# Layer 2's token rows in slot order: 16 direct stores in place of 16 scatters, no rows of zeros

## The chip, the core and the metric

One of the eight cores of a Trainium2 chip runs the kernel. The metric is the time of one execution on the device in microseconds (us), input in HBM to output in HBM. A core has five engines with a program each: PE (TensorE, matrix products; PEld is its load of weights), DVE (VectorE), ACT (ScalarE), POOL (GpSimd) and SP (SyncE, which here only issues transfers). Transfers run on 16 DMA engines; SP, ACT and POOL issue them. SBUF is the core's memory of 128 partitions, PSUM the one that PE writes.

## What is computed

Tokens pass through a retention (a linear attention with a decay for each head), a mixture of 8 experts without a limit, and a second mixture whose experts hold at most 384 tokens each, first come first served:

```python
for t in range(S):                                    # B=2, H=8, S=768, 64 wide
    state = gamma * state + einsum('bhd,bhe->bhde', k[:, :, t], v[:, :, t])
    y[:, :, t] = scale * einsum('bhd,bhde->bhe', q[:, :, t], state)
# _moe_ref: N=1536 tokens, D=512, E=8, F=1024
expert_idx = argmax(x @ w_gate);  gate_w = softmax(x @ w_gate)[expert_idx]
out[mask_e] = gate_w * (maximum(x[mask_e] @ w1[e], 0) @ w2[e])
# _moe2_ref: the same, but token i is kept only if its expert has had fewer than `capacity` tokens; else out[i] = 0
```

## The kernel before

**Three stages.** From 0 to about 66 us the retention runs over 12 tiles of 128 tokens (`for n in range(NT)`). PE, DVE and POOL work on tile n while SP loads the q, k and v of tile n+3 (`a_load`). Each tile ends as rows of 520 f32, 512 values of the token and its 8 logits for layer 1, which ACT stores to the DRAM array `x1d` (line 564). From 66 to about 250 us comes the first mixture (`li == 0`), from there to the end the second (`li == 1`). The two are called layer 1 and layer 2 here.

**One expert.** A layer takes its experts in an order found at run time and gives each a fixed number of slots (`CAPS`: 240, 220, 208, 200, 192, 188, 184, 176 in layer 1). So that PE works on full rows, an expert's tokens are gathered from DRAM by an indirect DMA on POOL (`take`, line 347): 128 rows and a rest of 48 to 112, called the halves r0 and r1. Weights and tokens are split into a high and a low part: SP loads f32 weights `st`, ACT makes `whi` (line 159), DVE makes `wlo = st - whi` (line 170). The hidden layer runs in four groups: PE makes `h` (800, 801), ACT copies `hb` (785), DVE adds into `hs` (786), ACT makes the high part of relu (811), DVE the low part (812), both into tile `h`. Then PE makes `y` from them (844, 845) in two passes, ACT copies `yb`, DVE adds `yt` (785, 786).

**Rows of layer 2.** `comb` brings `yt` of an expert back to rows: four matmuls into `cb` (1334), on DVE the logits (1340) times the gate (1342), on ACT the 512 values times the gate (1347) into `row`, one of four buffers. Then `scatter(x2d, ...)` (line 321, POOL) sends each row to `x2d` at its token's number; slots that hold no token have an index out of range and are left out. All this is in a list `pend`, of which `between` runs pieces inside the next expert: r0 of expert j in the first hidden group of expert j+1, r1 in the second. Only expert 7's two halves come after its own products. `rou` then ranks the rows for layer 2 (`route_tile`, lines 204 to 234) on DVE and PE.

**What else touches `x2d`.** Twelve stores of a tile of zeros clear it first (`clear`, line 661): seven in the retention behind a tile's loads, five inside layer 1's expert 0, all on SP. Layer 2 gathers from `x2d` by token, and 128 rows ahead of time (`early`) once expert 6's rows of layer 1 are in its order. Layer 2 scatters its results to `out` by token (`put_out`, `scatter`). The code under `late` and `dropped` handles overfull experts; with these inputs its loops run zero times.

**Order.** The programs of the engines are static. What stands in ACT's program runs in that order, so a DMA that ACT issues holds up what is behind it until it has been issued. `order` rows below show where things stand.

Of the kernel before, what the change touches and what calls it, by code (L numbers as in the profile page):

```python
# [36 lines left out]
WC = 1024  # L37
NZ = 7
NST = 4
# [6 lines left out]
def _consts(capacity):  # L46
    gamma = 1.0 - 2.0 ** (-5.0 - np.arange(H, dtype=np.float64))
    s = np.arange(P, dtype=np.float64)
    parts = []

    def put(name, a):
        a = np.asarray(a, dtype=np.float32).reshape(P, -1)
        lo = sum(x.shape[1] for x in parts)
        _C[name] = (lo, lo + a.shape[1])
        parts.append(a)

    put("mask", (s[:, None] <= s[None, :]))
# [12 lines left out]
    put("slot", np.stack([s, s + P], axis=1))  # L70
    put("caps", np.broadcast_to(np.minimum(np.array(CAPS), [[N], [capacity]]).reshape(1, -1), (P, 2 * E)))
# [8 lines left out]
def fused(ctx, tc, qT, kT, vkr, wg, w11, w12, w21, w22, cst, out, capacity):  # L80
# [7 lines left out]

    x1d = tc.dram_tile([N, RW], F32, name="x1d")
    x2d = tc.dram_tile([N, RW], F32, name="x2d")  # L90

# [160 lines left out]
    def finish_route(rt, li, mix=()):  # L252
# [59 lines left out]
        while mix:  # L312
            beside()
        return {"sel": sel, "order": order, "ns": ns, "ig": ig, "tk": tk, "isc": isc, "vl": vl}

# [24 lines left out]
    def put_rows(dst, index, rows):  # L340
        after_scatters(nc.gpsimd.indirect_dma_start(
            dst[:, :], bass.IndirectOffsetOnAxis(ap=index, axis=0), rows, None, bounds_check=N - 1,
            oob_is_err=False).ins, dst)

    def take(xd, index, cnt, pool=None, tag="rows", n=N):
# [125 lines left out]
    with tc.tile_pool(name="ap", bufs=3) as ap:  # L471
# [188 lines left out]
        def clear(t):  # L660
            nc.sync.dma_start(x2d[t * P:(t + 1) * P, :], zero)

        for n in range(NT):
# [37 lines left out]
            a_load(n + 3)  # L701
            if n < NZ:
                clear(n)
            step(n - 2, 0)
# [157 lines left out]

    def put_out(j, r, cnt, ps, gate, ix):
        ob = xp.tile([P, D], F32, tag="ob", name="ob", bufs=2)[:cnt]
        A.activation(ob, ps, AF.Copy, scale=gate)  # L865
        c = r * E + j
        scatter(out, ix["isc"][:cnt, c:c + 1], ob)

# [10 lines left out]
    def layer(li, xd, rin):  # L879
# [5 lines left out]
        gate = {0: [gates(r) for r in ([rows[0][0]], [rows[0][1]])]}  # L885
        x = {}
        got, go = ahead
# [32 lines left out]
        if li == 1:  # L920
            gate[0][0][0]()
            ps0 = mmtile("o")
            o_part(E * 8, P, h, [ps0], range(0, 6))
            gate[0][0] = gate[0][0][1]()
            x[0] = first_x(rows[0][1])
            o_part(E * 8, P, h, [ps0], range(6, KF))
            put_out(0, 0, P, ps0, gate[0][0][0], ix)

        def between(j, i):
# [43 lines left out]
        for j in range(E):  # L973
# [6 lines left out]
            for i in range(4):  # L980
# [28 lines left out]
                if j == 0 and i == 2:  # L1009
                    if li == 0:  # L1010
                        gate[0][0] = gate[0][0][1]()
                    gate[0] = gate[0][0] + gate[0][1][1]()
            gt = gate[j]
            if li == 0:
# [30 lines left out]
                def comb(r, cnt, j=j, yt=yt, gt=gt):  # L1045
# [29 lines left out]
            elif P < cap <= YC:  # L1075
# [11 lines left out]
                def back(r, cnt, j=j, yt=yt, gt=gt):  # L1087
                    p = mmtile("o")[:cnt]
                    for d in range(KD):
                        T.transpose(p[:, d * P:(d + 1) * P], yt[:, d, r * P:r * P + cnt], ident)  # L1090
                    put_out(j, r, cnt, p, gt[r], ix)

                pend.extend([lambda f=back, r=r, c=c: f(r, c) for r, c in halves(cap)])
            elif j + 1 == E and cap == P:
                ix2 = cp.tile([P, 2], I32, name="ix2")
                for i in range(2):
                    V.tensor_scalar(ix2[:, i:i + 1], ix["isc"][:, j:j + 1], 2.0, float(i), ALU.mult, ALU.add)
                ps = [mmtile("o")[:, 0:D // 2] for _ in range(2)]
# [15 lines left out]
            else:  # L1114
# [5 lines left out]
                for (r, cnt), p in zip(tiles, ps):  # L1120
                    put_out(j, r, cnt, p, gt[r], ix)
        if li == 0:
# [55 lines left out]
    def late(li, xd, rin, todo):  # L1178
# [24 lines left out]
        V.tensor_scalar(z, vl, -float(BIG), float(BIG), ALU.mult, ALU.add)  # L1203
        ig = rp.tile([P, 2], I32, tag="lig", name="lig")
        V.tensor_copy(ig[:, 0:1], tk)
        V.tensor_add(ig[:, 1:2], tk, z)
        rows = take(xd, ig[:, 0:1], P)
        first, second = gates([rows])
# [47 lines left out]
        if li == 0:  # L1256
            yt = xp.tile([P, KD, C0], F32, tag="yt", name="yt")
            A.copy(yt[:, :, :P], ps.rearrange("p (d c) -> p d c", d=KD))
            row, lg = combine(nc, pp, rp, yt[:, :, :P], iw[1], gt, P)
            put_rows(x2d, ig[:, 1:2], row)  # L1260
# [4 lines left out]
            pick, rank = route_tile(rt[1], lg, tk, vl, P, at=new)[:2]  # L1265
            pick()
            rank()
        else:
            ob = xp.tile([P, D], F32, tag="ob", name="ob", bufs=2)
# [4 lines left out]
    def dropped():  # L1274

        zero = rp.tile([P, RW], F32, tag="zero", name="zero", bufs=1)[:, 0:D]
        V.memset(zero, 0.0)
# [5 lines left out]
        for n in range(NT):  # L1283
# [3 lines left out]
            lg = rp.tile([P, E], F32, tag="dl", name="dl")  # L1287
            nc.sync.dma_start(lg, x2d[at * P:(at + 1) * P, D:RW])
            pick, rank = route_tile(route, lg, tok, None, P, at=0)[:2]
# [10 lines left out]
    with tc.If(nc.values_load(flag[0:1, 0:1], min_val=0, max_val=2) > 0):  # L1300
# [28 lines left out]
def combine(nc, pp, rp, xt, iw, gate, cnt, lg=None):  # L1329

    cb = pp.tile([P, 2, 512], F32, tag="cb", name="cb", bufs=1)[:cnt]
    for k in range(KD):
        lo = (k % 2) * (P + E)
        nc.tensor.matmul(cb[:, k // 2, lo:lo + P + E], xt[:, k, :], iw[:, k, :], start=True, stop=True)  # L1334
    row = rp.tile([P, RW], F32, tag="row", name="row", bufs=4)[:cnt]
    v = cb[:, :, 0:2 * (P + E)].rearrange("p i (j c) -> p i j c", j=2)
# [91 lines left out]
```

## Time and profile before

| | us |
|---|---|
| time, median of 3 runs (lowest to highest) | 422.86 (420.6 to 423.39) |
| the profiled execution's own time | 423.04 |
| its span, first to last recorded instruction | 421.3 |
| PE busy in the span | 408.0 (97%) |
| DVE busy | 319.4 (76%) |
| ACT busy | 238.6 (57%) |
| POOL busy | 98.1 (23%) |
| mean granted TensorE clock | 0.998 of full speed |

The span is the part that the trace shows; 423.04 - 421.3 = 1.74 us lie around it. In lists of instructions a row is: start, duration, engine, line, operation, tile written <- tiles read, and the shapes. Brackets at its end give the idle time of the engine before it and what released it. "x2" is two alike in one row.

### The profile page before, as it was taken

How to read it: one execution, taken by the hardware profiler on the slowest of the kernel's cores; microseconds unless marked ns; L12 is line 12 of the kernel's file. 1: busy time of each engine (PE TensorE's matmuls, PEld its weight loads, DVE VectorE, ACT ScalarE, POOL GpSimd, SP SyncE). 2: the span in 40 equal slices, each digit the busy share in tenths (PEclk: the TensorE clock that was granted, in tenths of full speed). 3: DMA queues.
4: the chain of work that ended last, by engine and by line, in shares of the span. 5: the costliest groups of instructions: out<-in, count | busy, mean ns of one | idle time of the engine just before them, and what ended most of it. 6: DMA issues, size and time to landing. Idle time of an engine off the chain costs nothing.

```text
span 421.3 us, 9473 instructions
## 1 busy us (share of the span) xinstructions
PE 408.0 (97%) x3403; PEld 382.0 (91%) x3403; DVE 319.4 (76%) x870; ACT 238.6 (57%) x485; POOL 98.1 (23%) x89
## 2 busy tenths in 40 slices
PE   8998989999999999999999999999999999999993
PEld 7887779999899999999999988999888999999993
DVE  3778787678989798989798867378576788887840
ACT  2111132567677676767665631557776678787650
POOL 2344313303023130404000204003221504021021
PEclk9999999999999999999999999999999999999999
DMA  8999983976667766767657903768867777778711
GB/s 309 397 389 385 344 325 99 345 262 206 237 222 232 242 211 235 237 226 233 225 178 222 330 10 78 308 220 269 293 219 256 229 247 261 243 240 269 233 42 33
DMA packets 32503, 100.45 MB, mean 238 GB/s; under 512 B 4669, under 2 KB 5181, under 8 KB 32448
## 3 DMA queue, kind: packets, MB, share of 16 engines
q1 hardware_dynamic: 25488, 82.74, 57.5%
q0 software_dynamic: 4656, 13.00, 9.0%
q10 hardware_dynamic: 2304, 4.02, 2.6%
q8 instruction: 29, 0.48, 0.4%
q14 instruction: 26, 0.21, 0.2%
HBM read 87.01 MB, written 12.99 MB: 237 GB/s over the span
## 4 chain that ended last, share of the span: by engine, by line
PE 74%; DMA 11%; DVE 6%; issue 3%; ACT 2%; SPq 1%; POOL 1%; POOLq 0%; ACTq 0%; DVEq 0%
PE h L800 16%; PE y L844 16%; PE h L801 7%; PE y L845 7%; PE h L434 5%; DMA st<-w 5%; PE cb L1334 4%; DMA vk<-vkr 3%; PE o L859 3%; PE o L861 3%; PE o L860 3%; PE tp L362 2%; DVE wlo L170 2%; DMA whole<-w 2%; DMA x1d<-row 1%
## 5 line engine op out<-in xcount | busy, mean ns | idle before, releaser
L170 DVE TENSOR_TENSOR wlo<-st,whi 128x1024 fp32r<-128x1024 f32 x120 | 145.0, 1216 | 2.5 <-ACT whi L159 2.5
L159 ACT CAST whi<-st 128x1024 fp32r<-128x1024 f32 x120 | 125.1, 1045 | 29.0 <-DMA st<-w 28.6
L844 PE MATMUL y<-h,whi 128*128 128x416 f32 (+9 forms) x384 | 117.2, 369 | 0.0
L800 PE MATMUL h<-x,whi 128*128 128x416 f32 (+9 forms) x384 | 114.5, 365 | 0.0
L845 PE MATMUL y<-h,wlo 128*128 128x208 f32 (+9 forms) x384 | 96.9, 252 | 0.0
L801 PE MATMUL h<-x,wlo 128*128 128x208 f32 (+9 forms) x384 | 96.7, 252 | 0.0
L844 PEld LDWEIGHTS y<-h,whi 128*128 128x128 f32 x384 | 72.1, 188 | 2.9 <-DVE rro L232 0.6
L800 PEld LDWEIGHTS h<-x,whi 128*128 128x128 f32 x384 | 72.1, 188 | 2.1 <-issue 0.6
L801 PEld LDWEIGHTS h<-x,wlo 128*128 128x128 f32 x384 | 73.4, 191 | 0.1
L845 PEld LDWEIGHTS y<-h,wlo 128*128 128x128 f32 x384 | 73.3, 191 | 0.0
L321 POOL DMA_INDIRECT x2d<-row,is x16 | 17.1, 1071 | 118.5 <-ACT row L1347 88.7
L812 DVE SCALAR_TENSOR_TENSOR h<-hs,h 128x416 fp32r<-128x416 f32 (+9 forms) x48 | 26.9, 561 | 19.1 <-ACT h L811 18.5
L321 POOL DMA_INDIRECT out<-ob,is x14 | 14.9, 1068 | 110.8 <-ACT ob L865 108.4
L811 ACT ACTIVATE h<-hs 128x416 fp32r<-128x416 f32 (+9 forms) x48 | 25.1, 523 | 25.5 <-DVE hs L786 25.4
L786 DVE TENSOR_TENSOR hs<-h,hb 128x208 f32<-128x208 f32 (+9 forms) x96 | 29.6, 347 | 6.8 <-ACT hb L785 6.8
L434 PE MATMUL h<-x,whole 128*128 128x128 f32 (+1 forms) x256 | 30.5, 277 | 0.0
L785 ACT COPY hb<-h 128x208 f32<-128x208 f32 (+9 forms) x96 | 27.0, 318 | 5.9 <-PE h L801 5.8
L1345 ACT COPY row<-cb 128x512 f32<-128x512 f32 x11 | 6.5, 586 | 41.1 <-DVE lgb L1340 25.0
L434 PEld LDWEIGHTS h<-x,whole 128*128 128x128 f32 x256 | 29.3, 192 | 0.3 <-issue 0.2
L347 POOL DMA_INDIRECT rows<-x1d,igs x14 | 24.3, 1735 | 9.2 <-issue 4.7
L786 DVE TENSOR_TENSOR yt<-y,yb 128x208 f32<-128x208 f32 (+9 forms) x48 | 15.0, 352 | 14.2 <-ACT yb L785 14.2
L859 PE MATMUL o<-whi,h 128*128 128x512 f32 (+1 forms) x64 | 24.3, 379 | 0.0
(198 smaller groups left out, 613.6 us busy)
## 6 DMA issues: line engine op xcount, KB each, us to landing
st<-w SPq DMA_DIRECT2D x120, 512.0 KB, 4.3
vk<-vkr SPq DMA_DIRECT2D x11, 512.0 KB, 6.0
whole<-w SPq DMA_DIRECT2D x8, 512.0 KB, 7.1
x2d<-zero SPq DMA_DIRECT2D x12, 260.0 KB, 7.6
qb<-qT SPq DMA_DIRECT2D x12, 256.0 KB, 5.7
x1d<-row ACTq DMA_DIRECT2D x11, 260.0 KB, 5.8
kt<-kT SPq DMA_DIRECT2D x11, 256.0 KB, 5.7
vk<-vkr ACTq DMA_DIRECT2D x1, 512.0 KB, 4.6
```

What stands on the lines that cost most here:

```text
L159: A.copy(hi, st)
L170: V.tensor_sub(lo, st, hi)
L321: ins = nc.gpsimd.indirect_dma_start(dst.rearrange("n (i d) -> (n i) d", i=parts) if parts > 1 else dst[:, :], bass.IndirectOffsetOnAxis(a ...
L434: T.matmul(ps[:, j], w[:, k, j % 2 * P:(j % 2 + 1) * P], x[:, k], start=k == 0, stop=k == KD - 1, skip_group_check=True)
L785: A.copy(b, ps[:, 1, :])
L786: V.tensor_add(out, ps[:, 0, :], b)
L800: T.matmul(ps, hi[:, k, fs], x[:, k, :, :cap], start=k == 0, stop=False, skip_group_check=True)
L801: T.matmul(ps[:, 0, :], lo[:, k, fs], x[:, k, 0, :cap], start=False, stop=k == KD - 1, skip_group_check=True)
L812: V.scalar_tensor_tensor(h[:, sl, 1, :cap], s, 0.0, h[:, sl, 0, :cap], ALU.max, ALU.subtract)
L844: T.matmul(ps[i], hi[:, ds], h[:, f, :, :cap], start=f == 0, stop=False, skip_group_check=True)
L845: T.matmul(ps[i][:, 0, :], lo[:, ds], h[:, f, 0, :cap], start=False, stop=f == KF - 1, skip_group_check=True)
L859: T.matmul(p, h[:, f, 0, ts_], hi, start=f == 0, stop=False)
```

## The change

A row of `x2d` no longer stands at its token's number but at its slot's: expert j's half r begins at row `OFF[j] + 128 r`, where `OFF` is the running sum of layer 1's slots (0, 240, 460, ... 1608). So `x2d` needs neither an index for the store nor zeros under it. What it needs is the token's number for the result, which goes into a new column 520; rows are 521 f32.

- `comb`: POOL's scatter is replaced by a POOL copy of the token numbers into the row's last column and a plain store, issued by ACT.
- `clear`, its tile of zeros and the 12 stores go.
- Layer 2: the routing's "token" of a row is now its row number (`con("row")`, 17 more columns in the constants), so that its gathers fetch slots; DVE makes the output index from the gathered column (`out_index`, one addition for each half of an expert).
- `early` gathers from the rows of experts 0 to 5 alone (`OFF[E - 2]`, 1248 rows).
- Overfull experts get rows behind 2048; that code isn't run here.

The diff, cut to what runs here:

```diff
+OFF = tuple(sum(CAPS[0][:j]) for j in range(E + 1))
+    put("row", s[:, None] + np.array([OFF[j] + r * P for r in range(2) for j in range(E)])[None, :])
-    x2d = tc.dram_tile([N, RW], F32, name="x2d")
+    x2d = tc.dram_tile([LATE + 4 * N, RW + 1], F32, name="x2d")
@@ take
-        t = (pool or xp).tile([P, RW], F32, tag=tag, name="rows", bufs=4)[:cnt]
+        t = (pool or xp).tile([P, RW + 1], F32, tag=tag, name="rows", bufs=4)[:cnt, 0:xd.shape[1]]
+        n = n or (N if xd is x1d else OFF[E])
@@ retention
-        zero = rp.tile([P, RW], F32, tag="zero", name="zero", bufs=1)
-        G.memset(zero, 0.0)
-            nc.sync.dma_start(x2d[t * P:(t + 1) * P, :], zero)
...
             a_load(n + 3)
-            if n < NZ:
-                clear(n)
@@ one layer
+    def out_index(rows, ix, j, r):
+        cnt = rows.shape[0]
+        c = r * E + j
+        t = xp.tile([P, 1], I32, tag="oi", name="oi", bufs=6)[:cnt]
+        V.tensor_add(t, rows[:, RW:RW + 1], ix["z"][:cnt, c:c + 1])
+        return t
...
-            if li == 0 and j == 0 and i < 2:
-                for t in range(NZ, NT)[3 * i:3 * i + 3]:
-                    clear(t)
...
-                early(rt[1], x2d, N)
+                early(rt[1], x2d, OFF[E - 2])
...
                 gate[j + 1] = gate[j + 1][1]()
+                if li == 1:
+                    to[j + 1] = [out_index(t, ix, j + 1, r) for r, t in enumerate(rows[j + 1])]
@@ comb
-                    scatter(x2d, ix["isc"][:cnt, c:c + 1], row)
+                    G.tensor_copy(row[:, RW:RW + 1], ix["tk"][:cnt, c:c + 1])
+                    at = OFF[j] + r * P
+                    nc.scalar.dma_start(x2d[at:at + cnt, :], row)
@@ rou
-                        steps[r] = route_tile(rt[1], lgs[r], ix["tk"][:cnt, c:c + 1], ix["vl"][:cnt, c:c + 1],
+                        steps[r] = route_tile(rt[1], lgs[r], con("row")[:cnt, c:c + 1], ix["vl"][:cnt, c:c + 1],
```

ACT's program in the first two hidden groups of layer 1's expert 3 (`row` is expert 2's row buffer, `h` expert 3's hidden layer), before:

```order
L785 COPY hb<-h 128x200 x2
L1347 ACTIVATE row<-cb,gt 128x512
L811 ACTIVATE h<-hs 128x2x200
L159 CAST whi<-st 128x1024
L785 COPY hb<-h 128x200 x2
L1347 ACTIVATE row<-cb,gt 80x512
L811 ACTIVATE h<-hs 128x2x200
L159 CAST whi<-st 128x1024
```

and with the change:

```order
L782 COPY hb<-h 128x200 x2
L1366 ACTIVATE row<-cb,gt 128x512
L1058 DMA x2d<-row 128x521
L808 ACTIVATE h<-hs 128x2x200
L163 CAST whi<-st 128x1024
L782 COPY hb<-h 128x200 x2
L1366 ACTIVATE row<-cb,gt 80x512
L1058 DMA x2d<-row 80x521
L808 ACTIVATE h<-hs 128x2x200
L163 CAST whi<-st 128x1024
```

In experts 1 to 7 a store stands between each evacuation of a row half and the high part of the hidden group; expert 7's own two stores follow its last evacuations.

POOL's program around the rows of experts 0 and 1 (`rows` are the gathered tokens of the experts ahead), before:

```order
L347 DMA rows<-x1d,igs_1223 128x520
L347 DMA rows<-x1d,igs_1223 80x520
L321 DMA x2d<-row,is_1235 1536x520 x2
L347 DMA rows<-x1d,igs_1223 128x520
L347 DMA rows<-x1d,igs_1223 72x520
L321 DMA x2d<-row,is_1235 1536x520 x2
```

and with the change:

```order
L352 DMA rows<-x1d,igs_1215 128x520
L352 DMA rows<-x1d,igs_1215 80x520
L1056 COPY row<-tk_1207 128x1
L1056 COPY row<-tk_1207 112x1
L352 DMA rows<-x1d,igs_1215 128x520
L352 DMA rows<-x1d,igs_1215 72x520
L1056 COPY row<-tk_1207 128x1
L1056 COPY row<-tk_1207 92x1
```

Two copies stand where two scatters stood, behind the gathers for two experts ahead.

SP's program at the start of layer 1's expert 0, before (`ISA` and `st<-w` are the steps of a weight load):

```order
L138 DMA st<-w 128x1024
L661 DMA x2d<-zero 128x520 x3
L138 ISA
L138 DMA st<-w 128x1024
L138 ISA
L138 DMA st<-w 128x1024
L661 DMA x2d<-zero 128x520 x2
L138 ISA
```

and with the change:

```order
L142 ISA
L142 DMA st<-w 128x1024
L142 ISA
L142 DMA st<-w 128x1024
L142 ISA
L142 DMA st<-w 128x1024
```

The weight loads follow one another.

## Rows read from the trace of the kernel before

**Rows 1.** Windows: length, busy us of PE, PEld, DVE, ACT, POOL, clock, DMA share, GB/s

```profile
40.00:50.00 10.00, 10.00 (x174) 8.58 (x173) 6.86 (x21) 1.37 (x4) 4.36 (x5) 1.00 0.98 337
...
140.00:160.00 20.00, 20.00 (x149) 19.60 (x148) 18.53 (x53) 13.44 (x26) 6.12 (x4) 1.00 0.67 222
...
273.00:410.00 137.00, 136.92 (x943) 128.85 (x942) 103.16 (x192) 97.74 (x190) 29.28 (x24) 1.00 0.70 234
410.00:421.30 11.30, 4.17 (x36) 3.97 (x34) 0.62 (x2) 0.95 (x2) 1.97 (x2) 0.92 0.09 31
```

**Rows 2.** Waits of PE: for what, us in total, times, longest

```profile
PE cb L1334 <- DVE xt L557: 1.5, 2, 1.0
```

**Rows 3.** Waits of DVE

```profile
DVE h L812 <- ACT h L811: 21.3, 28, 2.8
DVE yt L786 <- ACT yb L785: 14.2, 13, 2.3
```

**Rows 4.** Timeline of ACT, first two hidden groups of expert 3

```profile
141.98 0.69 ACT L1347 ACTIVATE row<-cb,gt 128x512 f32<-128x512 f32 x1 [0.85 <-DVE row L1340]
142.56 0.53 ACT L811 ACTIVATE h<-hs 128x400 fp32r<-128x400 f32 x1
...
146.10 0.53 ACT L811 ACTIVATE h<-hs 128x400 fp32r<-128x400 f32 x1
```

**Rows 5.** Timeline of DVE, the same groups, and the fourth

```profile
143.12 0.57 DVE L812 SCALAR_TENSOR_TENSOR h<-hs,h 128x400 fp32r<-128x400 f32 x1 [0.91 <-ACT h L811]
...
146.30 0.29 DVE L213 TENSOR_SCALAR roh<-rkey,rmk,vl 128x8 f16<-128x8 f32 x1
146.66 0.57 DVE L812 SCALAR_TENSOR_TENSOR h<-hs,h 128x400 fp32r<-128x400 f32 x1
...
152.51 0.57 DVE L812 SCALAR_TENSOR_TENSOR h<-hs,h 128x400 fp32r<-128x400 f32 x1
```

**Rows 6.** Timeline of PE, expert 3: first `y` product that reads group four

```profile
153.73 0.36 PE L844 MATMUL y<-h,whi 128*128 128x400 f32 x1
```

**Rows 7.** Timeline of DVE and PE, expert 7: the same two places

```profile
240.85 0.52 DVE L812 SCALAR_TENSOR_TENSOR h<-hs,h 128x352 fp32r<-128x352 f32 x1
...
241.76 0.35 PE L844 MATMUL y<-h,whi 128*128 128x352 f32 x1
```

**Rows 8.** Timeline of ACT, a store of the retention's rows

```profile
51.24 0.59 ACT L1345 COPY row<-cb 128x512 f32<-128x512 f32 x1 [4.96 <-DVE row L1340]
51.86 0.33 ACTq L564 DMA_DIRECT2D x1d<-row  x1
52.22 1.05 ACT L159 CAST whi<-st 128x1024 fp32r<-128x1024 f32 x1 [0.40 <-ACT row L1345]
```

**Rows 9.** DMA issues: times, KB each, median us to landing

```profile
x2d<-zero SPq DMA_DIRECT2D x12, 260.0 KB, 7.6
...
x1d<-row ACTq DMA_DIRECT2D x11, 260.0 KB, 5.8
...
x2d<-row,is POOLq DMA_INDIRECT x16, 3.2
```

**Rows 10.** Timeline: ACT in layer 1's expert 0, DVE in expert 6

```profile
83.87 1.05 ACT L159 CAST whi<-st 128x1024 fp32r<-128x1024 f32 x1 [2.85 <-DMA st<-w]
...
207.52 0.19 DVE L1340 TENSOR_REDUCE row<-cb 128x8 f32<-128x32 f32 x1 [0.26 <-PE ch L385]
```

**Rows 11.** Timeline of PE in expert 1, about the first `cb`

```profile
97.41 0.26 PE L801 MATMUL h<-x,wlo 128*128 128x220 f32 x1
97.82 0.72 PE L1334 MATMUL cb<-iw,yt 128*112 128x136 f32 x4
```

**Rows 12.** Timeline of POOL: scatters of expert 0's rows, gathers behind them

```profile
101.78 0.98 POOL L321 DMA_INDIRECT x2d<-row,is  x1 [2.65 <-DVE rmk L208]
103.06 1.54 POOL L347 DMA_INDIRECT rows<-x1d,igs  x1 [0.30 <-PE h L801]
```

**Rows 13.** Timeline of DVE, an operation on one column

```profile
140.64 0.15 DVE L767 TENSOR_SCALAR gs<-gs 128x1 f32<-128x1 f32 x1
```

More of the change, by code (lines that the diff above doesn't have):

```diff
@@ L29 @@
 RW = D + E
+OFF = tuple(sum(CAPS[0][:j]) for j in range(E + 1))
+LATE = 2048
 BIG = 1 << 20
@@ L37 @@
 WC = 1024
-NZ = 7
 NST = 4
@@ L70, in _consts @@
     put("slot", np.stack([s, s + P], axis=1))
+    put("row", s[:, None] + np.array([OFF[j] + r * P for r in range(2) for j in range(E)])[None, :])
+    put("late", LATE + 4 * s)
     put("caps", np.broadcast_to(np.minimum(np.array(CAPS), [[N], [capacity]]).reshape(1, -1), (P, 2 * E)))
@@ L89, in fused @@
     x1d = tc.dram_tile([N, RW], F32, name="x1d")
-    x2d = tc.dram_tile([N, RW], F32, name="x2d")
+    x2d = tc.dram_tile([LATE + 4 * N, RW + 1], F32, name="x2d")
+    lgd = tc.dram_tile([N, E], F32, name="lgd")
     def mmtile(name):
@@ L313, in finish_route @@
             beside()
-        return {"sel": sel, "order": order, "ns": ns, "ig": ig, "tk": tk, "isc": isc, "vl": vl}
+        return {"sel": sel, "order": order, "ns": ns, "ig": ig, "tk": tk, "isc": isc, "vl": vl, "z": z}
     scattered, gathers = {}, []
@@ L341, in put_rows, with take @@
         after_scatters(nc.gpsimd.indirect_dma_start(
-            dst[:, :], bass.IndirectOffsetOnAxis(ap=index, axis=0), rows, None, bounds_check=N - 1,
+            dst[:, :], bass.IndirectOffsetOnAxis(ap=index, axis=0), rows, None, bounds_check=dst.shape[0] - 1,
             oob_is_err=False).ins, dst)
-    def take(xd, index, cnt, pool=None, tag="rows", n=N):
-        t = (pool or xp).tile([P, RW], F32, tag=tag, name="rows", bufs=4)[:cnt]
+    def take(xd, index, cnt, pool=None, tag="rows", n=None):
+        t = (pool or xp).tile([P, RW + 1], F32, tag=tag, name="rows", bufs=4)[:cnt, 0:xd.shape[1]]
+        n = n or (N if xd is x1d else OFF[E])
         ins = nc.gpsimd.indirect_dma_start(
@@ L656, in fused @@
         a_decay(0)
-        zero = rp.tile([P, RW], F32, tag="zero", name="zero", bufs=1)
-        G.memset(zero, 0.0)
-        def clear(t):
-            nc.sync.dma_start(x2d[t * P:(t + 1) * P, :], zero)
         for n in range(NT):
@@ L861, in o_part, with put_out @@
                 T.matmul(p, h[:, f, 1, ts_], hi, start=False, stop=f == KF - 1)
-    def put_out(j, r, cnt, ps, gate, ix):
+    def out_index(rows, ix, j, r):
[4 more added lines that the diff above has]
+        return t
+    def put_out(r, cnt, ps, gate, index):
         ob = xp.tile([P, D], F32, tag="ob", name="ob", bufs=2)[:cnt]
         A.activation(ob, ps, AF.Copy, scale=gate)
-        c = r * E + j
-        scatter(out, ix["isc"][:cnt, c:c + 1], ob)
+        scatter(out, index[:cnt], ob)
     pend = []
@@ L885, in layer @@
         gate = {0: [gates(r) for r in ([rows[0][0]], [rows[0][1]])]}
-        x = {}
+        x, to = {}, {}
         got, go = ahead
@@ L924, in layer @@
             gate[0][0] = gate[0][0][1]()
+            to[0] = [out_index(rows[0][0], ix, 0, 0)]
             x[0] = first_x(rows[0][1])
             o_part(E * 8, P, h, [ps0], range(6, KF))
-            put_out(0, 0, P, ps0, gate[0][0][0], ix)
+            put_out(0, P, ps0, gate[0][0][0], to[0][0])
         def between(j, i):
@@ L1012, in layer @@
                     gate[0] = gate[0][0] + gate[0][1][1]()
+                    if li == 1:
+                        to[0].append(out_index(rows[0][1], ix, 0, 1))
             gt = gate[j]
@@ L1090, in back @@
                         T.transpose(p[:, d * P:(d + 1) * P], yt[:, d, r * P:r * P + cnt], ident)
-                    put_out(j, r, cnt, p, gt[r], ix)
+                    put_out(r, cnt, p, gt[r], to[j][r])
                 pend.extend([lambda f=back, r=r, c=c: f(r, c) for r, c in halves(cap)])
@@ L1096, in layer @@
                 for i in range(2):
-                    V.tensor_scalar(ix2[:, i:i + 1], ix["isc"][:, j:j + 1], 2.0, float(i), ALU.mult, ALU.add)
+                    V.tensor_scalar(ix2[:, i:i + 1], to[j][0], 2.0, float(i), ALU.mult, ALU.add)
                 ps = [mmtile("o")[:, 0:D // 2] for _ in range(2)]
@@ L1120, in layer @@
                 for (r, cnt), p in zip(tiles, ps):
-                    put_out(j, r, cnt, p, gt[r], ix)
+                    put_out(r, cnt, p, gt[r], to[j][r])
         if li == 0:
@@ L1203, in late @@
         V.tensor_scalar(z, vl, -float(BIG), float(BIG), ALU.mult, ALU.add)
-        ig = rp.tile([P, 2], I32, tag="lig", name="lig")
+        ig = rp.tile([P, 3], I32, tag="lig", name="lig")
         V.tensor_copy(ig[:, 0:1], tk)
-        V.tensor_add(ig[:, 1:2], tk, z)
-        rows = take(xd, ig[:, 0:1], P)
+        rows = take(xd, ig[:, 0:1], P, n=xd.shape[0])
+        V.tensor_add(ig[:, 1:2], tk if li == 0 else rows[:, RW:RW + 1], z)
         first, second = gates([rows])
@@ L1259, in late @@
             row, lg = combine(nc, pp, rp, yt[:, :, :P], iw[1], gt, P)
-            put_rows(x2d, ig[:, 1:2], row)
+            put_rows(lgd, ig[:, 1:2], lg)
+            V.tensor_copy(row[:, RW:RW + 1], tk)
+            V.tensor_add(ig[:, 2:3], lrow, z)
+            put_rows(x2d, ig[:, 2:3], row)
             new = rt[1]["n"]
@@ L1264, in late @@
             pushed(rt[1]["r"][:, new:], [P, NL], 1, "lpr")
-            pick, rank = route_tile(rt[1], lg, tk, vl, P, at=new)[:2]
+            pick, rank = route_tile(rt[1], lg, lrow, vl, P, at=new)[:2]
             pick()
             rank()
+            V.tensor_scalar(lrow, lrow, 4.0 * P, None, ALU.add)
         else:
@@ L1274, in dropped @@
     def dropped():
-        zero = rp.tile([P, RW], F32, tag="zero", name="zero", bufs=1)[:, 0:D]
+        zero = rp.tile([P, D], F32, tag="zero", name="zero", bufs=1)
         V.memset(zero, 0.0)
@@ L1287, in dropped @@
             lg = rp.tile([P, E], F32, tag="dl", name="dl")
-            nc.sync.dma_start(lg, x2d[at * P:(at + 1) * P, D:RW])
+            nc.sync.dma_start(lg, lgd[at * P:(at + 1) * P, :])
             pick, rank = route_tile(route, lg, tok, None, P, at=0)[:2]
@@ L1315, in fused @@
         V.tensor_scalar(rt[1]["S"], most, ident[:, 0:1], None, ALU.mult)
+        for j in range(E):
+            for r, cnt in halves(CAPS[0][j]):
+                c = r * E + j
+                lg = rp.tile([P, E], F32, tag="dl", name="dl")[:cnt]
+                nc.sync.dma_start(lg, x2d[OFF[j] + r * P:OFF[j] + r * P + cnt, D:RW])
+                put_rows(lgd, ixs[0]["isc"][:cnt, c:c + 1], lg)
+        lrow = cp.tile([P, 1], F32, name="lrow")
+        V.tensor_copy(lrow, con("late"))
         todo, reg = listed(0, ixs[0]["ns"])
@@ L1334, in combine @@
         nc.tensor.matmul(cb[:, k // 2, lo:lo + P + E], xt[:, k, :], iw[:, k, :], start=True, stop=True)
-    row = rp.tile([P, RW], F32, tag="row", name="row", bufs=4)[:cnt]
+    row = rp.tile([P, RW + 1], F32, tag="row", name="row", bufs=4)[:cnt]
     v = cb[:, :, 0:2 * (P + E)].rearrange("p i (j c) -> p i j c", j=2)
@@ L1357, in __init__ @@
         self.nc, self.rp, self.iw, self.gate, self.cnt = nc, rp, iw, gate, cnt
-        self.row = rp.tile([P, RW], F32, tag="row", name="row", bufs=4)[:cnt]
+        self.row = rp.tile([P, RW + 1], F32, tag="row", name="row", bufs=4)[:cnt]
         self.lg = self.row[:, D:RW]
```

## Prediction

> **What bounds the kernel now.** I read the table of windows first, to see which engine is full in which stage. In 40 to 50 us, inside the retention, PE is busy 10.00 of 10.00 us, although the DMA engines are as good as full too (share 0.98, 337 GB/s). In layer 1 (140 to 160) PE has 20.00 of 20.00 and DVE 18.53; in layer 2 (273 to 410) PE has 136.92 of 137.00 and DVE 103.16 [rows 1]. So PE's stream has no holes that could be closed, except at the start and in the last 11.3 us, where PE works 4.17 us and the last results go to `out`; the change touches nothing there. The list of PE's waits says the same: the longest sum is 1.5 us, and it waits for DVE [rows 2]. No DMA of zeros and no scatter appears in it. A gain can therefore come only from some tenths of a us; the question is what the change can hurt.
>
> So I read next what DVE waits for, since in layer 1 it is nearly as full as PE. Its largest wait is for ACT: `h` (812) waits for ACT's `h` (811), 21.3 us in 28 waits; the next is `yt` for ACT's `yb`, 14.2 us in 13 [rows 3]. The timelines of expert 3 show how. ACT evacuates `row` from 141.98 for 0.69 us, then makes the high part of `h` from 142.56 for 0.53, to 143.09; DVE stands idle 0.91 us and starts its part at 143.12, 0.03 us behind ACT [rows 4, 5]. In the second group ACT's part ends at 146.10 + 0.53 = 146.63, DVE starts at 146.66, and DVE's work before it ended at 146.30 + 0.29 = 146.59 [rows 4, 5]. So in both groups ACT sets the time, and the second has next to no reserve on DVE either. What is queued behind on DVE follows without further long gaps to the fourth group, at 152.51 to 153.08 [rows 5]; PE reads it at 153.73 [rows 6], so the reserve is 0.65 us. In expert 7 the same places are 240.85 + 0.52 = 241.37 and 241.76: 0.39 us [rows 7]. **Two loops run at one pace here**: PE without holes, and DVE with ACT right behind it.
>
> **The change, part by part.**
>
> *The 14 stores in experts 1 to 7.* This is the term that carries the sum. Each stands on ACT between the evacuation of a row half and the high part of `h`, in just the two groups in which DVE waits for that. Before, the same work was a scatter on POOL, off this path. The trace shows the same store on the same engine in the retention: the evacuation ends at 51.24 + 0.59 = 51.83, the issue takes 0.33 us from 51.86, and the next operation starts at 52.22 [rows 8], 0.39 us behind the evacuation. Without a store ACT's operations overlap: 811 starts at 142.56, while the evacuation ends at 142.67 [rows 4], 0.11 us earlier. A store thus costs 0.39 + 0.11 = 0.50 us; the lower end is the issue alone, 0.33. I take 0.50, since that row is the very pattern. Group one: 0.50. Group two: 0.50 less the 0.04 between DVE's free time and ACT's end, 0.46. Together 0.96 for each expert, 7 x 0.96 = 6.7 us of delay on the loop of DVE and ACT. Behind the store on ACT wait the high part of `h`, `whi` and `hb`; for these DVE waits, and for DVE's `h` PE.
>
> The loop gives little back: DVE has no long wait for PE in which to catch up. The largest that I find is 0.26 us in expert 6 [rows 10]. PE's lag at the end is the loop's delay less the reserve left in expert 7: 6.7 - 0.39 - 0.26 = 6.1 us.
>
> Expert 7's own two stores stand at the end of layer 1, where ACT waits for PE; I cost them at nothing, at most 2 x 0.50 = 1.0 us.
>
> *The 16 scatters that go.* About 1 us of POOL each (0.98 in the row), and the gathers behind them no longer queue: the one at 103.06 came up 0.30 us after it [rows 12]. POOL is busy 6.12 of 20 us in layer 1 [rows 1], and PE has no wait for gathers there, so the gain is nothing; that is also its lower end. The 16 small copies on POOL run while the row's products are still ahead; an operation of that size on DVE takes 0.15 us [rows 13], and the highest bound is what they replace. Where a store had to wait for its copy, it would go straight into the term above (rival D).
>
> *The 12 stores of zeros that go.* They move 12 x 260 KB, landing in 7.6 us [rows 9]. The seven in the retention lie under a PE that is busy all the time [rows 1]: nothing. The five in expert 0 compete with weight loads: ACT's `whi` waits 2.85 us for one at 83.87 [rows 10]. What of it reaches PE is seen at the first `cb` of expert 1: it starts 0.41 us after the product before it, where products of that kind stand 0.1 us apart at their closest: a gap of some 0.3 us [rows 11]. I take 0.3, with 0 below and 1.0 above.
>
> *Layer 2.* Sixteen additions of 128x1 on DVE, by that row 16 x 0.15 = 2.4 us [rows 13]; DVE has 137.00 - 103.16 = 33.8 us free in 273 to 410 [rows 1], so they are hidden; without that cover they would cost up to 2.4. Gathers by slot fetch as many rows as before, each 4 bytes longer: nothing. The early gather now waits for fewer rows: nothing, or an earlier landing that nobody waits for.
>
> **The sum.** 6.1 - 0.3 = 5.8 us on the profiled execution's 423.04 gives 428.8 us; that execution is 0.18 above the median of 422.86, so the median would be moved alike. With 0.33 for a store: 14 x 0.33 - 0.39 - 0.26 - 0.3 = 3.7, or 426.7. With expert 7's stores counted too: 429.8.
>
> **The rivals.**
>
> B, no change: the stores are absorbed. That would be so if ACT's sequencer issued the store while its evacuation still runs, so that the issue lies beside it, or if DVE had room that the trace hides. For it: ACT is only 13.44 of 20 us busy [rows 1]. Against it: the issue starts 0.03 us after the evacuation's end [rows 8], since it waits for that, and the idle time of ACT lies ahead of the evacuation (0.85 us), not behind it [rows 4]. Time: 423.04 - 0.3 = 422.7, from 422 to 424.
>
> The Trainium skill, page "DMA: Bandwidth & Descriptors", section "Issuing engines are not separate DMA queues", says that all issuers' transfers share the same 16 DMA engines and that the choice of issuer saves only the sequencer's issue time, "which is usually small relative to the DMA itself". By that rule the move from POOL to ACT is worth nothing and rival B holds; the trace agrees on the ratio (0.33 us of issue against 5.8 to landing), but what decides here is what stands behind the issue on ACT.
>
> C, faster: the zeros were a brake. In the retention 7 x 0.266 MB = 1.86 MB at 337 GB/s [rows 1] are 5.5 us of DMA time; were the loads the pace there, the end would come that much earlier, and with the stores absorbed the time would be 423.04 - 5.5 = 417.5. It decides from the point where PE waits for a load in 10 to 60 us. Against it: PE at 10.00 of 10.00 there [rows 1], and a list of waits headed by DVE [rows 2].
>
> D, slower still: the store waits on ACT for more than its evacuation, as for POOL's copy, which stands behind two gathers of 1 to 1.5 us [rows 12]. Each tenth of a us adds 14 x 0.1 = 1.4 us; at 0.2 us the time is 428.8 + 2.8 = 431.6. Against it: the gathers and copies stand an expert ahead of their use, some 20 us.
>
> **How the numbers follow.** The forecast (stores on the path) gets 0.60, with its own range 426 to 430.6; B 0.25; C 0.07; D 0.08. About 1% (4.2 us, to 427.1) is what a measurement of this kernel can tell from no change; of the forecast's 0.60 I put 0.10 below that line. Slower: 0.50 + 0.08 = 0.58; same: 0.25 + 0.10 = 0.35; faster: 0.07. The range runs from B's 422.3 to 430.6; it leaves out C, D and the edges, together about 0.2. I predict 428.8 us.
>
> **What would show it.** In the trace after: a store of about 0.33 us on ACT between `row` and `h` in experts 1 to 7, the next `h` about 0.4 us behind the evacuation's end; DVE's waits for ACT's `h` up by some 6 to 7 us from 21.3; holes in PE's stream from expert 1 or 2 on, in `y` where it reads group four, about 0.9 us for each expert, and none in layer 2. Wrong would be: DVE's waits grown but PE still at 20.00 of 20 (then the reserve was larger than two rows show); a store issued beside the evacuation (B); or PE's windows of 10 to 60 us shorter (C).

## The result and the profile after

The changed kernel takes 427.29 us (median of 4 runs, 427.02 to 427.81); the kernel before, on the same chips, 422.27. The ratio is 1.0124 with a 95% interval of 1.0085 to 1.0162: **slower by 1.2%, 5.0 us**. The forecast was 428.8, between 422.3 and 430.6, or 5.8 us more than the kernel before.

| | before | after |
|---|---|---|
| profiled execution's own time, us | 423.04 | 427.02 |
| its span | 421.3 | 425.2 |
| PE busy | 408.0 | 409.3 |
| POOL busy | 98.1 | 75.9 |
| mean granted TensorE clock | 0.998 | 0.998 |

PE does the same work, in a span 3.9 us longer. Windows of after (length, then busy us of PE, PEld, DVE, ACT, POOL, the clock, DMA share, GB/s), as in [rows 1]:

```profile
30.00:40.00 10.00, 9.79 (x168) 8.22 (x166) 9.13 (x32) 1.54 (x5) 3.29 (x5) 1.00 0.90 310
...
140.00:160.00 20.00, 19.75 (x142) 18.67 (x142) 17.36 (x51) 13.55 (x26) 1.87 (x3) 1.00 0.65 212
160.00:180.00 20.00, 19.59 (x140) 18.52 (x139) 16.53 (x51) 13.58 (x31) 2.88 (x4) 1.00 0.67 216
...
273.00:410.00 137.00, 137.00 (x946) 129.65 (x945) 105.94 (x207) 99.68 (x193) 26.60 (x23) 1.00 0.72 239
```

In layer 1 (140 to 180) PE has holes, where before it had 20.00 of 20; in layer 2 it has none. But a stretch of the retention has become fuller: in 30 to 40 us PE is busy 9.79 us, where before it was

```profile
30.00:40.00 10.00, 8.51 (x147) 7.20 (x146) 9.32 (x31) 1.37 (x4) 3.27 (x4) 1.00 1.03 386
```

The waits of DVE after, as in [rows 3], and then two of PE's that were not in its list before:

```profile
DVE h L809 <- ACT h L808: 28.7, 35, 1.8
DVE yt L783 <- ACT yb L782: 12.5, 13, 2.3
```

```profile
PE rk L224 <- DVE hs L783: 1.3, 5, 0.3
PE y L841 <- DVE hs L783: 1.1, 2, 0.7
```

DVE waits 7.4 us longer for ACT's `h` (28.7 against 21.3; the forecast had 6 to 7), and PE now waits for DVE. These sums cover the whole kernel. In the seven experts that hold the stores (94 to 252 us) the same wait reads, before and after:

```profile
DVE h L812 <- ACT h L811: 6.3, 7, 0.9
```

```profile
DVE h L809 <- ACT h L808: 14.8, 14, 1.5
```

There it grew by 8.5 us, 0.61 for each store, while DVE's wait for `yb` in that stretch fell from 7.7 to 5.3 us. The timeline of ACT in the same two groups of expert 3 as [rows 4]:

```profile
142.05 0.69 ACT L1366 ACTIVATE row<-cb,gt 128x512 f32<-128x512 f32 x1 [1.02 <-DVE row L1359]
142.81 0.33 ACTq L1058 DMA_DIRECT2D x2d<-row  x1
143.19 0.54 ACT L808 ACTIVATE h<-hs 128x400 fp32r<-128x400 f32 x1 [0.45 <-ACT row L1366]
```

and of DVE, as in [rows 5]:

```profile
143.77 0.57 DVE L809 SCALAR_TENSOR_TENSOR h<-hs,h 128x400 fp32r<-128x400 f32 x1 [1.48 <-ACT h L808]
...
147.86 0.58 DVE L809 SCALAR_TENSOR_TENSOR h<-hs,h 128x400 fp32r<-128x400 f32 x1 [0.62 <-ACT h L808]
```

The evacuation ends at 142.74, the store is issued from 142.81 to 143.14, and `h` starts at 143.19, 0.45 us behind the evacuation's end where it had begun 0.11 ahead of it. DVE's idle time grew from 0.91 to 1.48 in the first group (0.57) and from almost nothing to 0.62 in the second.

How this adds up is seen by following one product, the first `y` that reads group four. In expert 1 it stood at 108.66 before:

```profile
108.66 0.47 PE L844 MATMUL y<-h,whi 128*128 128x440 f32 x1
```

and in experts 1, 3 and 7 after:

```profile
107.54 0.47 PE L841 MATMUL y<-h,whi 128*128 128x440 f32 x1
...
154.34 0.45 PE L841 MATMUL y<-h,whi 128*128 128x400 f32 x1
...
247.00 0.35 PE L841 MATMUL y<-h,whi 128*128 128x352 f32 x1
```

Against before, PE is 1.1 us ahead in expert 1, 0.6 behind in expert 3 (153.73 in [rows 6]) and 5.2 behind in expert 7 (241.76 in [rows 7]). So there are two movements: some 6.3 us are lost between experts 1 and 7, and a lead of about 1 us was there before. Followed product by product, PE loses next to nothing in expert 1, whose two stores use up its reserve, and about 1.1 us (0.9 to 1.3) in each of the six experts behind it.

The lead has two parts. One comes out of the retention: at 70 us the same product of PE, first before and then after, stands 0.57 us earlier.

```profile
70.50 1.50 PE L374 MATMUL tp<-ones 128*128 128x128 f16 x24
```

```profile
69.93 1.50 PE L379 MATMUL tp<-ones 128*128 128x128 f16 x24
```

The other, about 0.4 us, comes at the first `cb` of expert 1 that [rows 11] shows, where the gap of 0.3 us is closed:

```profile
96.74 0.26 PE L798 MATMUL h<-x,wlo 128*128 128x220 f32 x1
96.84 1.09 PE L1353 MATMUL cb<-iw,yt 128*112 128x136 f32 x8
```

### The profile page after: what moved, and what is told of

Same layout as the page of the kernel before. It is cut to its first block, busy times and chain, and to the rows that moved or that the text cites. A ratio compares the mean times of both kernels' runs of the same rounds, so it can differ in the third digit from the quotient of the medians.

```text
span 425.2 us, 9446 instructions
## 1 busy us (share of the span) xinstructions
PE 409.3 (96%) x3403; PEld 381.6 (90%) x3403; DVE 318.7 (75%) x885; ACT 239.3 (56%) x485; POOL 75.9 (18%) x88
## 4 chain that ended last, share of the span: by engine, by line
PE 58%; DVE 21%; DMA 7%; ACT 5%; issue 4%; SPq 2%; ACTq 1%; POOL 1%; POOLq 0%
PE y L841 14%; DVE wlo L174 9%; PE h L797 8%; PE h L439 7%; PE y L842 6%; PE h L798 3%; DMA vk<-vkr 3%; DVE hs L783 3%; DVE h L809 3%; PE o L856 3%; PE o L858 3%; PE o L857 3%; ACT h L808 2%; DMA whole<-w 2%; ACT row L1366 2%
## 5 line engine op out<-in xcount | busy, mean ns | idle before, releaser
L163 ACT CAST whi<-st 128x1024 fp32r<-128x1024 f32 x120 | 125.1, 1046 | 22.2 <-DMA st<-w 22.2
L841 PE MATMUL y<-h,whi 128*128 128x416 f32 (+9 forms) x384 | 118.9, 373 | 1.4 <-DVE hs L783 1.1
L352 POOL DMA_INDIRECT rows<-x1d,igs x14 | 18.9, 1346 | 99.2 <-ACT gx L758 94.9
L325 POOL DMA_INDIRECT out<-ob,oi x14 | 14.2, 1016 | 111.7 <-ACT ob L869 109.2
L856 PE MATMUL o<-whi,h 128*128 128x512 f32 (+1 forms) x64 | 24.2, 378 | 0.0
L858 PE MATMUL o<-whi,h 128*128 128x512 f32 (+1 forms) x64 | 23.4, 366 | 0.0
```

The costliest lines, as they stand in the source:

```text
L163: A.copy(hi, st)
L841: T.matmul(ps[i], hi[:, ds], h[:, f, :, :cap], start=f == 0, stop=False, skip_group_check=True)
L856: T.matmul(p, h[:, f, 0, ts_], hi, start=f == 0, stop=False)
L858: T.matmul(p, h[:, f, 1, ts_], hi, start=False, stop=f == KF - 1)
```

## Experiments: what a store on ACT costs

**The stores behind `h`.** Only their place in ACT's program changes.

```diff
-                    nc.scalar.dma_start(x2d[at:at + cnt, :], row)
+                    owed.append((x2d[at:at + cnt, :], row))      # expert 7: issued at once, as before
...
         A.activation(h[:, sl, 0, :cap], s, AF.Relu)
+        while owed:
+            nc.scalar.dma_start(*owed.pop(0))
```

> The changed kernel, with the 14 stores of experts 0 to 6 issued on ACT right behind the high part of `h` instead of ahead of it; bytes, issuer and number of stores stay. Theory (the place on ACT is the cost): in the changed kernel PE's lag against before goes from -1.1 us at 100 us to +5.3 at 250, that is 6.4 us; without it the time is 427.3 - 6.4 = 420.9 us, DVE's waits for ACT's `h` fall from 28.7 to about 21 us. Rival (the stores' traffic, the copies on POOL or the new gathers slow layer 1): stays within 1 us of 427.3.

Measured: 420.86 us, ratio to before 0.9979 (0.9949 to 1.0009). DVE's waits for ACT's `h` are 19.9 us. Against the change's 1.0124 this is 1.45%, 6.1 us (6.4 between the medians). ACT in expert 3:

```profile
143.13 0.53 ACT L810 ACTIVATE h<-hs 128x400 fp32r<-128x400 f32 x1
143.31 0.33 ACTq L812 DMA_DIRECT2D x2d<-row  x1
143.68 1.05 ACT L163 CAST whi<-st 128x1024 fp32r<-128x1024 f32 x1
```

The issue (143.31 to 143.64) lies inside the run of `h` (143.13 to 143.66). The same 14 stores cost nothing here: their traffic, POOL's copies and the new gathers are not what makes the change slow.

**One group later, but still ahead of `h`.** This asks which part of a store costs, the issue or its wait.

```diff
+        before = owed[:]
+        owed.clear()
         run_pend()
+        for dst, row in before:
+            nc.scalar.dma_start(dst, row)
         A.activation(h[:, sl, 0, :cap], s, AF.Relu)
```

> The changed kernel, each store issued one hidden group later on ACT, still directly ahead of the high part of `h`, so that the evacuation that it reads ended some 4 us before. Number, issuer and bytes stay. Theory W (a store costs because it waits for the evacuation right in front of it, and the next operation can't start until it is issued; an issue whose data is ready goes beside the operation before): 420.9 us, as with the store behind `h`. Rival I (the issue holds ACT for its 0.33 us wherever it stands ahead of `h`): 14 x 0.33 = 4.6 us on top of 420.9, less some 0.4 of reserve: 425.

Measured: 420.20 us, ratio 0.9963 (0.9917 to 1.0009). The second group of expert 3:

```profile
143.37 0.68 ACT L1375 ACTIVATE row<-cb,gt 80x512 f32<-80x512 f32 x1 [1.03 <-DVE row L1368]
143.45 0.33 ACTq L813 DMA_DIRECT2D x2d<-row  x1
143.95 0.53 ACT L814 ACTIVATE h<-hs 128x400 fp32r<-128x400 f32 x1
```

The store of the other half is issued while this half's evacuation runs, and `h` starts 0.10 us before that ends, as it does without a store. Theory W holds: **the issue is free when it can run beside an operation that is under way, and on the path when it reads what the operation right in front of it writes.** In the second case three things follow one another: the end of the evacuation, the issue, the next start.

**Two stores in a row.**

```diff
                     nc.scalar.dma_start(x2d[at:at + cnt, :], row)
+                    nc.scalar.dma_start(rd[at:at + cnt, :], row)
```

> The changed kernel, each of the 16 stores issued twice in a row on ACT (the second into a DRAM array that nobody reads). Theory (the issue itself lies on the path of ACT, DVE and PE once it can't run beside an operation): 14 x 0.33 to 14 x 0.40 us more, 432 to 433 us. Rival (the cost is the wait for the evacuation alone, a second issue runs beside something): 427.3. Rival (the traffic is the cost): also 432 or more, but with weights late (ACT's waits for `st` well over 22 us).

Measured: 436.74 us, ratio 1.0346 (1.0322 to 1.0370), 9.4 us above the change, more than any theory had said. ACT in expert 3, and the second stores as a group (duration in ns, least, median, most):

```profile
144.98 0.35 ACTq L1059 DMA_DIRECT2D x2d<-row  x1
145.36 1.56 ACTq L1060 DMA_DIRECT2D rd<-row  x1
146.97 0.54 ACT L809 ACTIVATE h<-hs 128x400 fp32r<-128x400 f32 x1 [2.06 <-issue]
```

```profile
L1060 ACTq DMA_DIRECT2D rd<-row x16: 263/452/1565, 96.0 to 266.9; - x16
```

Behind a first store that had to wait, the second can't hide either, although its data is ready. It takes 0.45 us in the median and up to 1.56, while the first takes 0.34 in the median (0.32 to 0.51). The gaps on ACT ahead of `h`, like the 2.06 us here, sum to 15.0 us over the 14 places, against 6.7 with one store: 8.4 of the 9.4 us. The profile does not settle the last 1.0: TensorE's granted clock, 1.00 from 220 to 240 us with one store, had a mean of 0.91 there in this execution (the lower level, 1.2 GHz, in 229 to 231), and that may be part of it. Why one issue took 1.56 us stays open. ACT's waits for `st` are 20.4 us, under the 22.2 of the change, so it is not late weights.

**The stores on other engines.** On POOL (`nc.gpsimd.dma_start`):

> The changed kernel, with the 16 plain stores issued by POOL instead of ACT. Theory (the place on ACT is the cost): 420.9 us, as with the store behind `h`; POOL has room, about 1 us for each store as for a scatter. Rival (traffic or plain stores as such): about 427. Second rival (on POOL the store waits for the row with the gathers queued behind it, which then come late): 422 to 425, with PE waiting for `x`.

Measured: 420.80 us, ratio 0.9978 (0.9945 to 1.0010). On SP (`nc.sync.dma_start`):

> The changed kernel, with the 16 stores issued by SP. SP's program has the weight loads in order, and a store waits there for its row. Theory: ACT's path is as in the kernel before, 420.9 us, as far as weights are loaded an expert ahead. Rival (the weight loads queue behind a waiting store and come late): 422 to 426, with ACT's waits for `st` above 22 us and PE waiting for weights.

Measured: 421.79 us, ratio 0.9983 (0.9955 to 1.0010). In neither does layer 1 lose time: PE has 149.84 and 149.85 of 150 us in 100 to 250. SP's weight loads don't suffer from the stores among them (ACT waits 19.7 us for `st`). The three runs with the stores off ACT's path, on ACT behind `h`, on POOL and on SP, agree to within 1 us. The Trainium skill says that the choice of issuer saves only the sequencer's time to initiate the DMA, usually small relative to the DMA itself (page "DMA: Bandwidth & Descriptors", section "Issuing engines are not separate DMA queues"). As a duration that is so here (0.33 us), but through its place the issue cost 1.45% of the kernel.

**The whole row work behind `h`.** If ACT's `h` should not wait, why not put the evacuation behind it too?

```diff
-        run_pend()
         A.activation(h[:, sl, 0, :cap], s, AF.Relu)
         V.scalar_tensor_tensor(h[:, sl, 1, :cap], s, 0.0, h[:, sl, 0, :cap], ALU.max, ALU.subtract)
+        run_pend()
```

> The changed kernel, with the whole row work of a group (evacuation, store, logits, ranking) put behind both parts of `h`, on ACT and DVE. Theory: ACT's `h` is no longer behind the row's evacuation nor the store, so DVE's idle of 1.48 and 0.62 us in the first two groups of an expert goes, even the 0.9 of the kernel before; PE is then the only limit: 420.9 us, at best 0.5 below. Rival: the rows come later, the ranking matmuls (`rk`) wait, and PE loses about 0.5 us for each expert: 424.

Measured: 441.63 us, ratio 1.0471 (1.0405 to 1.0536). Both the theory and its rival were far off. The waits of DVE:

```profile
DVE h L808 <- ACT h L807: 30.3, 50, 1.5
...
DVE hs L783 <- ACT hb L782: 14.2, 16, 2.1
```

and two places of expert 3:

```profile
147.21 0.57 DVE L808 SCALAR_TENSOR_TENSOR h<-hs,h 128x400 fp32r<-128x400 f32 x1 [0.61 <-ACT h L807]
...
150.36 0.64 DVE L783 TENSOR_TENSOR hs<-h,hb 128x200 f32<-128x200 f32 x2 [1.08 <-ACT hb L782]
```

DVE now waits for `h` in every group of experts 1 to 7, 0.56 to 0.64 us (50 waits in all, not 35): the logits and the ranking that stood between `hs` and `h` on DVE had filled the time that ACT takes to make `h`. The sum of this wait is only 1.6 us larger than in the change (28.7). More comes from `hb`, 14.2 us where the change has 6.3: the evacuation, moved back, stands ahead of ACT's next `hb`, for which DVE waits 1.08 us. The rival's wait came too, PE for `rk` 5.7 us where the change has 1.3. How these add up to 14.3 us was not taken apart. In a loop of two engines that hand over to each other, work "in the way" on the one can be the cover of the other.

## Experiments: what the zeros cost

All 12 stores of zeros put back, into an array that nobody reads:

> The changed kernel, with the tile of zeros and the 12 stores of zeros put back at their old places (into a DRAM array that nobody reads). Theory (the zeros cost the retention 1.1 us that I had put at nothing, by making v and k land later): 427.3 + 1.1 = 428.4, PE again waits about 1 us for `xt` at 30 to 40 us, POOL's waits for `vk` rise from 17 to about 22 us. Rival (zeros are hidden, the gain at 40 us is chance of one execution): 427.3.

Measured: 428.60 us, ratio 1.0160 (1.0111 to 1.0209). Then in two parts, the seven of the retention alone:

> The changed kernel with only the seven stores of zeros in the retention put back. From the run with all 12, whose PE stream lagged the changed kernel's by 1.6 us at 40 us but only 0.5 at 66: theory (the zeros make v late, POOL's product of v then falls beside DVE's wide f16 operations, and most of that lag is taken back where PE waits for the early gather anyway): 1.6 us later at 40 us, about 0.5 at 66, time 427.8. Rival (all of the 1.3 us come from the retention): 428.6.

Measured: 428.56 us, ratio 1.0161 (1.0141 to 1.0182). And the five of expert 0 alone:

> The changed kernel with only the five stores of zeros in layer 1's expert 0 put back. Theory (they make weights late there, as the wait of 2.85 us for `st` in the kernel before shows; PE's stream with all 12 lost another 1.0 us between 100 and 120 us): even with the changed kernel to 100 us, 1.0 us behind from 120 on, time 428.3. My prediction put it at 0.3, with 1.0 as the upper bound: then 427.6.

Measured: 427.42 us, ratio 1.0125 (1.0105 to 1.0146).

So 1.3 us (between the medians; 1.5 by the ratios) belong to the seven stores in the retention: the rival was right there. On one chip the two parts don't overlap, 428.33 to 429.18 against 426.64 to 427.69 us. To the five in expert 0 nothing can be put down that these times show; 1.0 us was too much, and 0.3 can't be told from nothing. The profiled execution with all 12 had shown a lag of 1.0 us between 100 and 120; in the one with five alone there is none, so one execution's lag was a poor guide there. Nor was the gap ahead of the first `cb` of expert 1 the zeros' doing alone: with the five put back it is closed as well. Why it is, stays open.

```profile
97.17 0.26 PE L805 MATMUL h<-x,wlo 128*128 128x220 f32 x1
97.27 1.09 PE L1363 MATMUL cb<-iw,yt 128*112 128x136 f32 x8
```

Why the retention loses shows in the profiles. POOL waits for v and k (before; after; the seven put back):

```profile
POOL vp L498 <- DMA vk<-vkr: 22.3, 10, 5.4
```

```profile
POOL vp L503 <- DMA vk<-vkr: 17.2, 8, 5.4
```

```profile
POOL vp L504 <- DMA vk<-vkr: 21.0, 9, 5.5
```

and where POOL's product `vp` (1.04 us) then lies, first in the kernel before (POOL, DVE, PE in turn), then after (DVE, POOL):

```profile
32.39 1.04 POOL L498 TENSOR_TENSOR vp<-vk,cs 128x512 f32<-128x512 f32 x1 [2.60 <-DMA vk<-vkr]
...
32.48 1.60 DVE L622 TENSOR_SCALAR bR<-iota,r 128x256 f16<-128x256 f16 x2
...
34.56 1.17 PE L1334 MATMUL cb<-iw,xt 128*128 128x136 f32 x8 [1.00 <-DVE xt L557]
```

```profile
32.26 0.86 DVE L627 TENSOR_SCALAR bR<-iota,r 128x256 f16<-128x256 f16 x2
...
33.00 1.04 POOL L503 TENSOR_TENSOR vp<-vk,cs 128x512 f32<-128x512 f32 x1
```

and with the seven put back (POOL, then DVE):

```profile
32.64 1.04 POOL L504 TENSOR_TENSOR vp<-vk,cs 128x512 f32<-128x512 f32 x1 [1.93 <-DMA vk<-vkr]
...
32.95 1.39 DVE L628 TENSOR_SCALAR bR<-iota,r 128x256 f16<-128x256 f16 x2
```

With zeros on the queues, v lands later, and `vp` of this tile runs beside DVE's two `bR` (work on the ranks of the tokens), which then take 1.60 or 1.39 us instead of 0.86. The values `xt` behind them come late, and PE waits 1.0 us for `xt`, the largest item of [rows 2]; after, its waits for `xt` sum to 0.2. All the profiles agree. In the three with zeros in the retention POOL waits 21.0 to 22.6 us for v and k, `bR` takes 1.27 to 1.60 us and the longest wait of `cb` for `xt` is 0.9 to 1.1; in the ten without, these are 11.9 to 17.3, 0.85 or 0.86, and 0.3 at most.

A `vp` also falls beside DVE's first work on the ranks, in every one of these profiles, with or without zeros. Without them in the retention (the five in expert 0 put back):

```profile
29.12 1.04 POOL L504 TENSOR_TENSOR vp<-vk,cs 128x512 f32<-128x512 f32 x1 [0.17 <-POOL wm L535]
...
29.20 1.01 DVE L595 TENSOR_TENSOR bk<-lgb,bm 128x32 f32<-128x32 f32 x1
```

This operation takes 0.19 us in the profile after, where no `vp` is beside it; here it ends with `vp` (30.21 against 30.16). So the effect is strong there, but it is not what sets the runs with zeros apart. The Trainium skill says this of such pairs (page "SBUF — State Buffer", section "Who interferes with whom"): DVE operations with two inputs in SBUF, or in a two-port mode, share a port pair with GpSimd, and the one that comes second is blocked until the first is done. These rows agree.

## The stores off the path, and two weight loads held

The stores come into play only in layer 1; ahead of it, without the zeros, PE reaches the end of the retention early and waits there for the early gather: 1.1 us in the profile of the change and 2.3 us in the profile with the stores behind `h`, in which PE's clock also fell to a mean of 0.81 of full speed in 60 to 66 us, in 64 to 66 to the lower of its two levels (0.50, or 1.2 GHz), after PE had stood nearly idle (busy 0.15 of 2.40 us in 60 to 62.4). What made it fall is not shown: with the whole row work behind `h` PE waited 2.5 us for the same gather, and the clock stayed at 1.00. So two weight loads were held until that gather has landed:

```diff
                 for _ in range(4):
                     load_whole()
-                refill(2)
...
                 early(rt1, x1d, nb * P)
+                held[6] = held[7] = gathers[-1]
+                refill(2)
```

> The changed kernel with the stores behind `h`, and two weight loads of 0.5 MB at the end of the retention held back until layer 1's early gather has landed. In the run with the stores behind `h`, PE waited 2.3 us for that gather (landing 6.7 us), so that the 1.1 us which the missing zeros had brought were lost again there, and the granted clock fell to 0.81 in 60 to 66 us. Theory (the loads delay the gather): it lands 1.5 to 2.5 us earlier, PE's wait falls under 1 us, time 418.5 to 419.5. Rival (the gather is late for its own issue, or the held weights are missed at 70 to 80 us): 420.9 or above.

Measured: 421.03 us, ratio 0.9961 (0.9942 to 0.9981), on a chip where before took 422.67: 0.4% faster than the kernel before and 1.6% faster than the change. The gather landed in 3.7 us instead of 6.7, and PE's wait for it is gone from its list of waits in the profile, as the theory had it. But the time is the rival's (420.9 or above) and not 418.5 to 419.5: without the hold the ratio was 0.9979 (0.9949 to 1.0009), so a gain from the hold itself is not shown. The same hold with the stores one group later:

> The changed kernel with each store one hidden group later on ACT, and the two weight loads at the end of the retention held back until the early gather has landed. Theory (the two edits act in different stages: the store's place in layer 1, the load on the gather at 60 us): at or a little below both runs that have one of them (420.2 and 421.0), 419 to 420.5, faster than the kernel before by 0.5 to 0.8%. Rival (the gather's wait was chance of the profiled executions): 420.2, as without the hold.

Measured: 421.53 us, ratio 0.9995 (0.9970 to 1.0020): not faster than before. The forecast of 419 to 420.5 was missed. In its profile:

```profile
PE tp L382 <- DMA rows<-x1d,ig: 2.9, 1, 2.9
```

```profile
66.00:70.00 4.00, 4.00 (x49) 3.86 (x47) 3.49 (x17) 0.60 (x1) 1.48 (x2) 1.00 0.06 12
66.00:80.00 14.00, 11.12 (x113) 10.94 (x112) 8.04 (x23) 5.03 (x8) 4.32 (x4) 1.00 0.57 195
```

In this execution PE waits 2.9 us, up to 72.92, for the next gather (`ig`) instead. The held loads are not in its way: it is issued at 68.22, from 66 to 70 us the DMA engines are nearly idle (share 0.06), and SP issues the next weight load at 72.99. Why it is late stays open. What is shown is the stores' part; at the end of the retention single executions differ by a few us, for reasons that these runs don't separate.

## Why the prediction was right

**The path: right, and in part by luck so near in size.** The forecast had 0.50 us for a store in the first group and 0.46 in the second, 6.7 us on the loop, and 6.1 for PE after the reserves. Measured are 6.1 us (ratios) or 6.4 (medians) of time. The price of one store was a little low: 0.57 and 0.62 us of DVE's idle time in expert 3, 8.5 us in the 14 places. What the loop gives back was low as well: put at 0.39 + 0.26 us, while DVE's wait for `yb` alone fell by 2.4 in that stretch. The two errors nearly cancel. A pattern of the same kernel in another stage, [rows 8], still priced the store to within 0.06 us on ACT (0.45 us behind the evacuation where it showed 0.39). Where the price comes from was told right too: the issue waits for the evacuation. The experiments with the store one group later and behind `h` leave nothing else. Rival B's mechanism, an issue beside a running operation, is real, only not where the store stood.

**Where PE loses it: half right.** I had named the `y` product that reads group four. Its reserve in expert 3 went from 0.65 to 0.05 us (DVE's part ends at 153.72 + 0.57 = 154.29, PE reads at 154.34). In expert 7, where I had expected the reserve of 0.39 us to be used up, 0.31 are left (246.16 + 0.53 = 246.69, PE reads at 247.00):

```profile
153.72 0.57 DVE L809 SCALAR_TENSOR_TENSOR h<-hs,h 128x400 fp32r<-128x400 f32 x1
...
246.16 0.53 DVE L809 SCALAR_TENSOR_TENSOR h<-hs,h 128x352 fp32r<-128x352 f32 x1
```

PE's waits also stand at `rk`, the ranking products, and at the first `y` product. The loss of about 1.1 us for each expert is spread over several places with a small reserve.

**The zeros: wrong.** The step "the seven in the retention lie under a PE that is busy all the time: nothing" fell. I read the window of 40 to 50 us, where PE is full; the one before it had 1.5 us of holes. The list of PE's waits showed them, and I took "it waits for DVE" as a proof that no transfer was behind it. The chain has four links: zeros, v late on POOL, POOL beside DVE, DVE late for PE. The five in expert 0 were put at 0.3 us, and no cost of theirs can be measured. Together the term is 1.3 to 1.5 us instead of 0.3. That is not all of the 1.5 us by which 428.8 was too high. Half of them is the starting point: the profiled execution's 423.04, where the kernel before has a median of 422.27. The terms themselves gave 5.8 us more, and 5.0 were measured (5.2 by the ratio): zeros 1.0 to 1.2 us too small, less what the stores cost beyond 6.1. Rival C (the zeros were a brake) was right in direction, and far too large at 5.5 us.

**The small terms: right.** The copies on POOL, 0.18 us each, hold up nobody; the additions on DVE in layer 2 are hidden (PE 137.00 of 137.00); no gain from gathers without scatters ahead of them shows. POOL is 22 us less busy, for no gain. Rival D did not come: in all 14 places the store is issued 0.07 us behind the evacuation's end. The upper end of the range, 430.6, was not worked out from the terms; they reach 429.8.

## What to carry to other kernels

A DMA that an engine issues is a step of that engine's program: price it by its place. If it reads what the operation in front of it has just written, what follows waits for the write's end and the issue; behind the next operation the same issue was free here. Before moving work from an idle engine to one in the critical loop, look at the reserve of the hand-over behind it: none here, DVE was waiting for that very operation.

When an engine waits for another, follow that one's lateness back one or two steps before calling a transfer hidden.

## What was not expected of the hardware

- A DVE operation of 0.19 us took 1.01 us beside a POOL product of 1.04 us, ending with it; two others took 1.60 instead of 0.86.
- Of two stores issued in a row by ACT the second took 0.45 us in the median and up to 1.56, the first 0.34 in the median.
- A plain store issued by POOL took it 0.59 us in the median (0.53 to 0.61), an indirect one of the kernel before 1.02 (0.91 to 1.95).
